# Chunk 2 of a delta-rule attention kernel: the products with the state issued ahead of the joins, and three smaller moves

## The chip, the cores and the metric

The kernel runs on one core of a Trainium2 chip. The metric is the device time of one execution in microseconds, here the median of ten runs. The engines work side by side, each in its own fixed order: TensorE (PE, with its weight loads shown as PEld), VectorE (DVE), ScalarE (ACT), GpSimd (POOL) and SyncE (SP), which issues most of the DMA transfers. ScalarE issues the transfers of the output. An engine goes on to its next instruction only when the one before it could start, so an instruction that waits holds back all that stand behind it.

## The reference

A delta-rule linear attention over 4 batches, 8 heads, 768 steps and a head size of 48, and behind it a two-layer feed-forward network on the 3072 rows of 8 x 48 = 384 values, with an inner size of 2048 and exact GELU:

```python
k_n = k / (np.linalg.norm(k, axis=-1, keepdims=True) + 1e-06)
state = np.zeros((B, H, D, D), dtype=np.float32)
for t in range(S):
    kt, vt, bt = (k_n[:, :, t], v[:, :, t], beta[:, :, t, None])
    y[:, :, t] = np.einsum('bhd,bhde->bhe', q[:, :, t], state)
    v_old = np.einsum('bhde,bhd->bhe', state, kt)
    state = state + bt[:, :, :, None] * np.einsum('bhd,bhe->bhde', kt, vt - v_old)
...
h = x @ w_in
g = 0.5 * h * (1.0 + erf(h * inv_sqrt2))
return (g @ w_out).astype(np.float32)
```

## The kernel before

The 768 steps are cut into 12 chunks of 64. Inside a chunk the recurrence is solved at once: with the Gram matrix of the chunk's keys, a triangular matrix of 64 x 64 per head is inverted, and the inverse Z is applied to what is left of the values once the state has been subtracted. Chunks go in pairs, called groups; group 1 is chunks 2 and 3. The 32 heads of a chunk lie in two units of 128 partitions (two batches each, `p`), 8 heads in the free direction.

**Inverse of a group.** `eliminate_steps` works on VectorE alone. The two 32 x 32 diagonal blocks of each triangle are eliminated in 30 steps of two instructions (L443, L445), in `Nu`. Three transpositions then lead back to the layout of the matmuls: the first (L454) into `XM`, the second and the third (both L458) into the columns 32 to 63 and 0 to 31 of `Zf`. The third is followed by four clearings on POOL (L470).

**Joins.** The off-diagonal block of each inverse is made by two small matmuls per head. `join_run` does a level 0 (off-diagonal Gram `G` times `XM`; VectorE scales the product by the step sizes `gm` and puts it back into `XM`, four instructions of L541) and a level 1 (`XM` times `Zf`; ScalarE copies it into `Zf`, four instructions of L512). `join_steps` makes three runs: the first joins are level 0 for the group's first chunk; the second are level 1 of the first chunk, in turn with level 0 of the second; the third are level 1 of the second.

**A chunk with the state.** `against_state` multiplies keys and queries of the chunk with the state (`psK`, L603; "K S" for the keys' part), copies the queries' part to `y` on ScalarE (L610) and forms `W` on VectorE: the keys' part less `V` (L611), times `gm` (L612). `solve` multiplies by Z (`psU`, L628) and ScalarE copies the result in eight pieces (L634). `use` makes the outputs and the change of the state (`psY`, L646 and L655), VectorE adds the change (L660) and forms `x` (L669), `turn` transposes `x` (`psX`, L690) for the network. `queries` is the product of queries and keys, masked by L403. `grams` makes the Gram matrix of a chunk (`psG`, L367) and has it copied into `G` and `diag`; for chunks above 3 these copies are put into a list by `put_off`, and `copy_out` issues them at a time of their own and holds them in the order of the program.

**The network** follows one chunk behind: `fc1` (`psH`, L713, with GELU on ScalarE, L715) and, for chunks 0 and 1, `fc2` (`psO`, L726); from chunk 2 on a second layer with seven products in place of eight (L751). It fills TensorE between the small matmuls of the next chunk. While chunk 2 of the attention is worked on, the network is at chunk 1.

**PSUM.** There are eight banks. `dn` is a buffer of two banks, there twice, for `psK`, `psU`, `psY`, `psG` and `psJ` of level 0. `mlp` is one bank, twice, for the network. From the end of chunk 1 on (`late`) there is one bank `sq`, for transposed blocks and `psJ` of level 1, and one bank `z`, used by one of the seven products (`psZ2`, L773). A new tile in a buffer waits until the last reader of the tile before it is done.

**Order.** A list `plan` gives each step a time on a scale in units of chunks; `at` spreads a list of steps over an interval, and `emit` issues all steps by time. VectorE keeps exactly this order (`manual_schedule`). A scheduler reorders the other engines by its own estimates, but for what `together` binds: it makes the matmuls of its steps follow each other without a break. For chunk 2, the plan has the elimination of group 1 with its three transpositions at 1.75 to 2.45, the three runs of joins at 2.64 to 2.77, the query products at 2.725, and the steps with the state at 2.76 to 2.985.

**Loads.** The keys of a chunk are loaded once whole as `Kn` (for the sum of squares, `ksq` on ScalarE, L278, and its reduction on VectorE, L281), once as blocks `Kb` (transposed on VectorE into `Kt`, L352), and once as `Kp`. Each load waits until the buffer's last reader is done, and the loads of SyncE go out one behind the other.

Of the kernel before, what the change touches and what calls it, by code (L numbers as in the profile page):

```python
# [8 lines left out]
F32 = mybir.dt.float32  # L9
# [7 lines left out]
def kernel(  # L17
# [28 lines left out]
    nc = tc.nc  # L46
# [6 lines left out]
    NA = B // 2  # L53
# [15 lines left out]
    def dn(name):  # L69
        return ps.tile([128, 2, 512], F32, tag="dn", name=name)  # L70

    def sq(name, *shape):
        return small[0].tile([128, *shape], F32, tag="sq", name=name)
# [17 lines left out]
    tiles = {}  # L91
# [149 lines left out]
    def decode_steps(first, last):  # L241
        def start_(n):
            begin(n)
            exponents(n)

        steps = [(0.6, start_, first), (1.5, mantissas, first)]
        for n in range(first, last):
            if n + 1 < last:
                steps += [(0.6, start_, n + 1), (1.9, signed, n), (1.5, mantissas, n + 1)]
        return steps + [(1.9, signed, last - 1)]  # L250
# [121 lines left out]
    def grams(us):  # L372
        g = us[0].c // 2
        psG = products(us, 0)
        if us[0].t == 0:
            Gs[g] = (wk if g else su).tile([128, NU, HB], F32, tag="G", name="G", bufs=1)
        span = slice(us[0].t * H, (us[-1].t + 1) * H)
        put = put_off if us[0].c > 3 else lambda name, dst, src: nc.scalar.copy(dst, src)
        put("gram", heads(Gs[g][:, span]), psG[:, :, :, HB:C])
        if g > 0:  # L380
            if us[0].t == 0:
                Ds[g] = wk.tile([128, NU, HB], F32, tag="diag", name="diag", bufs=1)
            put("gram", heads(Ds[g][:, span]), psG[:, :, :, 0:HB])
            for p in range(2):
                lower = slice(p * C + HB, (p + 1) * C)
                put("gram", Ds[g][lower, span], Gs[g][lower, span])
# [128 lines left out]
    def join_run(g, ts0, ts1):  # L515

        xm, zf, off = XMs[g], Zf[g % 2], Gs[g]
        gm = gms[g].rearrange("q t h -> q (t h)")
        sets = []
        for level, ts in enumerate((ts0, ts1)):  # L520
            if ts:
                psJ = sq("psJ", 512) if level else dn("psJ")[:, 0]
                sets.append((level, ts[0] * H, psJ.rearrange("q (k n) -> q k n", n=2 * HB)))
        for k in range(H):
            for p in range(2):
                for level, u0, psJ in reversed(sets):
                    us = slice(u0 + 2 * k, u0 + 2 * k + 2)
                    rows = slice(p * C + level * HB, p * C + (level + 1) * HB)
                    nc.tensor.matmul(psJ[HALF[p], k, :],  # L529
                                     lhsT=(xm if level else off)[rows, us, :],  # L530
                                     rhs=zf[rows, us, HB:C] if level else xm[rows, us, :],
                                     start=True, stop=True)
        for level, u0, psJ in sets:
            for p in range(2):
                for e in range(2):
                    us = slice(u0 + e, u0 + 2 * H, 2)
                    at_ = p * C + e * HB
                    src = psJ[at_:at_ + HB, :, e * HB:(e + 1) * HB]
                    if level == 0:
                        low_ = slice(p * C + HB, (p + 1) * C)  # L540
                        nc.vector.tensor_tensor(  # L541
                            xm[low_, us, :], src,
                            gm[low_, us].unsqueeze(2).to_broadcast([HB, H, HB]), op=ALU.mult)
                    else:
                        put_off("join", zf[p * C:p * C + HB, us, HB:C], src)
# [41 lines left out]
    def against_state(us):  # L587

        for u in us:
            u.W = wk.tile([128, H, D], F32, tag="W", name="W")  # L590
            u.y = None
            if u.c == 0:
                nc.gpsimd.tensor_tensor(u.W, u.V,
                                        ng[:, u.a].unsqueeze(2).to_broadcast([128, H, D]),
                                        op=ALU.mult)
                continue
            u.psK = dn("psK")[:, :, 0:2 * NP * D].rearrange("q r (x j d) -> q x r j d", x=2, d=D)
            for x in range(2):
                for j in range(NP):
                    for r, p in QUADS:  # L600
                        rows = slice(r * C, r * C + D)
                        to = HALF[p ^ (j % 2)] if x and u.c > 1 else HALF[p]
                        nc.tensor.matmul(u.psK[to, x, r, j, :], lhsT=(u.Qt if x else u.Kt)[rows, p, j, :],  # L603
                                         rhs=St[rows, u.a, p, j, :], start=True, stop=True)
        for u in us:
            if u.c == 0:
                continue
            gm = gms[u.c // 2][:, u.t]
            u.y = wk.tile([128, H, D], F32, tag="y", name="y")
            nc.scalar.copy(heads(u.y), u.psK[:, 1])  # L610
            nc.vector.tensor_tensor(heads(u.W), u.psK[:, 0], heads(u.V), op=ALU.subtract)  # L611
            nc.vector.tensor_tensor(u.W, u.W, gm.unsqueeze(2).to_broadcast([128, H, D]),  # L612
                                    op=ALU.mult)
# [226 lines left out]
    def at(first, last, steps):  # L840

        total, done, timed = sum(s[0] for s in steps), 0.0, []
        for w, *step in steps:
            timed.append((first + (last - first) * (done + 0.5 * w) / total, step))
            done += w
        return timed
# [109 lines left out]
    def late():  # L956
# [3 lines left out]
        for a in range(NA):  # L960
# [3 lines left out]
            for c in range(5, NC, 2):  # L964
                tiles[c, a].Kb = Kb

    plan = [at(c + 1 + 0.25 * (c == 1), c + 2 + 0.25 * (c == 0), ffn_steps(c)) for c in range(NC)]
    plan += [at(0.985, 1.26, decode_steps(3, n_in)), at(1.26, 1.65, decode_steps(n_in, NW)), at(1.66, 1.67, [(1.0, late)])]
    plan += [at(0.98, 0.985, [(1.0, load, 3)]),
             at(1.02, 1.1, [(1.0, join, 0, range(NA, 2 * NA), level) for level in range(2)]),  # L970
]
    sums = [(1.0, sum_of_squares, tiles[c, a], h) for c in (2, 3) for a in range(NA) for h in range(H)]
    plan += [at(1.08, 1.5, sums), at(1.51, 1.511, [(1.0, prep, c) for c in (2, 3)]), at(1.65, 1.655, [(1.0, finish_both)]), at(2.97, 2.971, [(1.0, finish, 4)]), at(2.725, 2.726, [(1.0, queries, third)]),
             at(1.12, 1.6, state_steps(1)),
             at(1.75, 2.45, eliminate_steps(1)),
             at(2.64, 2.77, [s for j in join_steps(1) for s in ((1.0, together, j), (0.0, copy_out, "join", 4))]), at(2.76, 2.985, state_steps(2)),
             at(2.72, 2.721, [(1.0, prep, 4)]), at(2.8, 2.9, [(1.0, grams, [tiles[4, a] for a in range(NA)]), (0.0, copy_out, "gram", 4)])]
    plan += [at(0.995, 1.0, [(1.0, load_v, 2)]), at(2.98, 2.981, [(1.0, sums_of_w)]), at(3.1, 3.11, [(1.0, last_sum_of_w)])]
    plan += [at(c - 0.4, c - 0.3, v_steps(c)) for c in range(4, NC)]
    plan += [at(2.08, 2.44, [(1.0, scale_head, tiles[c, a], h)  # L980
# [24 lines left out]
    for w in range(3, NC):  # L1005
        two_ahead = w + 2 < NC
        if w % 2:
            if w == 3:
                plan += [at(w + 0.09, w + 0.092, [(1.0, transposed, u, (1,)) for u in fourth]
                            + [(1.0, together, *gram(5))])]  # L1010
                plan += spread("gram", 4, w + 0.093)
            plan += [at(w + 0.25, w + 0.95, state_steps(w, (), query(w)))]
            if two_ahead:
                rows = eliminate_steps(w // 2 + 1)
                plan += [at(w - 0.16, w - 0.15, [(1.0, prep, w + 2)]),
                         at(w, w + 0.01, [(1.0, finish, w + 2)]),
                         at(w + 0.13, w + 0.18, rows[:2]), at(w + 0.18, w + 0.36, rows[2:14]),
                         at(w + 0.4, w + 1.06, rows[14:-3]), at(w + 1.07, w + 1.2, rows[-3:])]
        else:
            j0, j1, j2 = join_steps(w // 2)  # L1020
            plan += [at(w + 0.23, w + 0.232, [(1.0, together, j0, *query(w))]),
                     at(w + 0.3, w + 0.301, [(1.0, together, j1, *gram(w + 2))]),
                     at(w + 0.35, w + 0.97, state_steps(w, (j2,), gram(w + 3)))]
            plan += spread("join", 2, w + 0.32, w + 0.355)
            plan += spread("join", 4, w + 0.455)
            if two_ahead:
                plan += spread("gram", 1, w + 0.385, w + 0.42, w + 0.54, w + 0.58)
                plan += spread("gram", 1, w + 0.66, w + 0.661, w + 0.7, w + 0.701)
                plan += [at(w + 0.59, w + 0.591, [(1.0, prep, w + 2)]),
                         at(w + 0.9, w + 0.91, [(1.0, finish, w + 2)])]  # L1030
# [32 lines left out]
```

## Time and profile before

| | us |
|---|---|
| median of 10 runs | 661.91 |
| lowest and highest | 660.45, 663.54 |
| the profiled execution | 662.46 |
| its span in the profile | 660.7 |
| TensorE busy in the span | 634.9 |
| VectorE busy in the span | 457.3 |

The span goes from the first to the last instruction of the program; 1.8 us of the profiled execution lie around it. All times in the text below that are points on a line, such as "at 150.13", are microseconds from the start of the span. In the views an entry such as `128x256 f32 x24` counts instructions as the profiler sees them: an fp32 matmul of the program is two. An idle time in brackets at the end of a timeline's row is that before its first instruction, with the engine and line that ended it; `issue` means that the profile shows nothing that was waited for.

### The profile page before, as it was taken

The numbers are of one execution on the slowest core, as the hardware profiler recorded it, in microseconds if no ns is written. First come the engines' busy times: TensorE is split into PE (matmuls) and PEld (weight loads), VectorE is DVE, ScalarE is ACT, GpSimd is POOL, SyncE is SP. The second block draws the span as 40 slices with busy tenths as digits, with TensorE's granted clock in tenths as the row PEclk, the third lists the DMA queues.
The fourth block names the chain that finished last, engine by engine and source line by source line (L and its number), as shares of the span: only waits on it lengthen the run. The fifth ranks groups of instructions, "written<-read, shape, count | busy, mean of one in ns | idle before, by whom it ended". The sixth has DMA issues, their size and how long they took to land.

```text
span 660.7 us, 20457 instructions
## 1 busy us (share of the span) xinstructions
PE 634.9 (96%) x8902; PEld 558.1 (84%) x8902; DVE 457.3 (69%) x941; ACT 230.2 (35%) x625; POOL 80.2 (12%) x82
## 2 busy tenths in 40 slices
PE   6778999999999999999999999999999999999997
PEld 5666777766689989889989989989989989989997
DVE  6999999996789855778855778855778844325022
ACT  3367745613542136132136132136132133131220
POOL 4041300104111011301011301011301010000000
PEclk9965999999999999999999999999999999999999
DMA  9795655303523223521233510212300210100101
GB/s 138 161 267 162 128 151 162 49 0 53 86 37 60 52 37 53 94 39 20 55 39 52 98 36 20 50 20 41 60 17 18 52 16 3 25 2 2 24 1 25
DMA packets 158426, 39.68 MB, mean 60 GB/s; under 512 B 150016, under 2 KB 153216, under 8 KB 158336
## 3 DMA queue, kind: packets, MB, share of 16 engines
q1 hardware_dynamic: 152464, 33.40, 26.5%
q10 hardware_dynamic: 5872, 4.97, 3.3%
q8 instruction: 70, 1.15, 0.7%
q14 instruction: 20, 0.16, 0.1%
HBM read 33.62 MB, written 4.72 MB: 58 GB/s over the span
## 4 chain that ended last, share of the span: by engine, by line
PE 85%; DVE 9%; ACT 3%; issue 2%; DMA 1%; SPq 0%; ACTq 0%; DVEq 0%
PE psH L713 36%; PE psX L751 12%; PE psY L751 12%; PE psO L726 5%; PE psZ L751 4%; PE psK L603 3%; PE psG L367 3%; PE psJ L529 3%; PE psU L628 2%; PE psY L646 2%; DVE tmp L443 2%; DVE Nu L445 2%; PE psY L655 1%; DVE w_e L235 1%; ACT U L634 1%
## 5 line engine op out<-in xcount | busy, mean ns | idle before, releaser
L713 PE MATMUL psH<-xT,w_in_sb 128*128 128x256 f32 x1152 | 260.1, 384 | 2.7 <-ACT G L715 1.6
L713 PEld LDWEIGHTS psH<-xT,w_in_sb 128*128 128x128 f32 x1152 | 217.3, 191 | 34.7 <-ACT G L715 3.4
L715 ACT ACTIVATE G<-psH 128x256 f32<-128x256 f32 x192 | 73.2, 382 | 179.0 <-PE psH L713 161.8
L445 DVE TENSOR_TENSOR Nu<-Nu,tmp 128x30 f32<-128x30 f32 (+9 forms) x180 | 61.5, 341 | 6.2
L443 DVE TENSOR_TENSOR tmp<-Nu 128x30 f32<-128x30 f32 (+9 forms) x180 | 62.1, 345 | 5.0
L751 PE MATMUL psX<-w_out_sb,G 128*128 128x192 f32 x320 | 55.8, 328 | 0.0
L751 PE MATMUL psY<-w_out_sb,G 128*128 128x192 f32 x304 | 54.1, 330 | 1.1
L691 ACT COPY xT<-psX 128x384 f32<-128x384 f32 x24 | 11.4, 478 | 124.3 <-PE psX L690 123.6
L751 PEld LDWEIGHTS psX<-w_out_sb,G 128*128 128x128 f32 x320 | 52.4, 190 | 0.6
L751 PEld LDWEIGHTS psY<-w_out_sb,G 128*128 128x128 f32 x304 | 49.1, 190 | 3.2 <-DVE u L797 3.2
L760 DVE TENSOR_TENSOR S<-G 128x512 f32<-128x512 f32 x20 | 13.8, 691 | 45.9 <-ACT G L715 45.5
L306 POOL TENSOR_TENSOR n<-n,half 128x16 f32<-128x16 f32 x10 | 29.4, 2937 | 128.2 <-DVE n L281 107.9
L726 PE MATMUL psO<-w_out_sb,G 128*128 128x384 f32 x128 | 44.5, 493 | 0.0
L611 DVE TENSOR_TENSOR W<-psK,V 128x384 f32<-128x384 f32 x22 | 12.2, 554 | 36.7 <-ACT y L610 36.7
L726 PEld LDWEIGHTS psO<-w_out_sb,G 128*128 128x128 f32 x128 | 23.5, 190 | 14.1 <-DVE w_out_sb L236 0.5
L634 ACT COPY U<-psU 64x192 f32<-64x192 f32 x96 | 30.0, 312 | 9.4 <-PE psU L628 8.3
L470 POOL MEMSET Zf<- 32x512 f32 x23 | 12.4, 540 | 160.4 <-DVE Zf L458 159.4
L765 DVE TENSOR_TENSOR G<-G 128x512 f32<-128x512 f32 x20 | 13.8, 692 | 25.7 <-PE psX L751 25.7
L669 DVE TENSOR_TENSOR x<-psY,y 64x192 f32<-64x192 f32 x80 | 28.2, 353 | 0.9
L751 PE MATMUL psY<-T,G 128*128 128x192 f32 x160 | 28.2, 330 | 0.0
L751 PE MATMUL psZ<-T,S 128*128 128x192 f32 x160 | 28.1, 329 | 0.0
L751 PE MATMUL psX<-T,G 128*128 128x192 f32 x160 | 28.1, 329 | 0.0
(141 smaller groups left out, 860.0 us busy)
## 6 DMA issues: line engine op xcount, KB each, us to landing
Kp<-in_k_dram SPq DMA_DIRECT2D x76, 96.0 KB, 3.2
w_out_sb<-in_moe_w_in_dram SPq DMA_DIRECT2D x24, 256.0 KB, 4.0
V<-in_v_dram SPq DMA_DIRECT2D x48, 96.0 KB, 3.1
out_dram<-o_sb ACTq DMA_DIRECT2D x46, 96.0 KB, 2.2
w_raw<-in_moe_w_out_dram SPq DMA_DIRECT2D x10, 384.0 KB, 4.9
Zf<-in_moe_w_out_dram SPq DMA_DIRECT2D x6, 384.0 KB, 3.8
Qp<-in_q_dram SPq DMA_DIRECT2D x64, 32.0 KB, 2.1
Qp<-in_q_dram SPq DMA_DIRECT2D x16, 96.0 KB, 4.3
```

The costliest lines, as they stand in the source:

```text
L306: nc.gpsimd.tensor_tensor(flat, flat, half, op=ALU.pow)
L367: nc.tensor.matmul(psG[HALF[p], r, i * NP + j, :], lhsT=u.Kt[rows, p, j, :], rhs=(u.Qt if x else u.Kt)[rows, p, j, :], start=True, stop=True)
L443: nc.vector.tensor_tensor(tmp, nu[:, j + 1:, j:j + 1].to_broadcast([128, n, j]), nu[:, j:j + 1, 0:j].to_broadcast([128, n, j]), op=ALU.mult)
L445: nc.vector.tensor_tensor(nu[:, j + 1:, 0:j], nu[:, j + 1:, 0:j], tmp, op=ALU.add)
L529: nc.tensor.matmul(psJ[HALF[p], k, :], lhsT=(xm if level else off)[rows, us, :], rhs=zf[rows, us, HB:C] if level else xm[rows, us, :], sta ...
L603: nc.tensor.matmul(u.psK[to, x, r, j, :], lhsT=(u.Qt if x else u.Kt)[rows, p, j, :], rhs=St[rows, u.a, p, j, :], start=True, stop=True)
L634: copy(pairs(u.U[HALF[p]], s), u.psU[HALF[p ^ s], p])
L669: nc.vector.tensor_tensor(dst, src, pairs(u.y[HALF[p ^ s]], s), op=ALU.add)
L713: nc.tensor.matmul(psH, lhsT=w_in_sb[:, f // 2, m, f % 2 * 128:(f % 2 + 1) * 128], rhs=xTs[c][:, m, :], start=(m == 0), stop=(m == NM - 1))
L715: nc.scalar.activation(G[:, f, :], psH, ACT.Gelu)
L726: nc.tensor.matmul(u.psO, lhsT=G[:, f, u.a * 128:(u.a + 1) * 128], rhs=w_out_sb[:, f, :], start=(f == 0), stop=(f == NF - 1))
L751: nc.tensor.matmul(ps_, lhsT=lhs[:, f, :], rhs=rhs[:, f, :], start=first and f == 0, stop=f == FH - 1, skip_group_check=not first)
```

## The change

Five things change, all but the second in chunk 2's part of the plan or next to it.

1. `against_state` is cut in two. For chunk 2 it only issues its matmuls, at 2.6 of the plan's scale, ahead of the first joins; the copies to `y` and the forming of `W` become a function `subtract`, called at 2.711.
2. `psJ` of level 0 is put into the bank `z` in place of a `dn` buffer, in all groups that use `join_run`.
3. The third back transposition of group 1 (the second L458, with the clearing on POOL) is issued behind the first joins with their L541 (2.661), at 2.662.
4. The second and third joins are at 2.7 and 2.75, and the sums of squares of chunk 4 at 2.73; the rest of the steps with the state follow from 2.8.
5. The copies of the Gram matrices of chunks 4 and 5 are no longer put off: they are issued where the Gram matrix is made, and the scheduler places them.

```diff
-        put = put_off if us[0].c > 3 else lambda name, dst, src: nc.scalar.copy(dst, src)
+        put = put_off if us[0].c > 5 else lambda name, dst, src: nc.scalar.copy(dst, src)
...
-                psJ = sq("psJ", 512) if level else dn("psJ")[:, 0]
+                psJ = small[0].tile([128, 512], F32, tag="sq" if level else "z", name="psJ")
...
                         nc.tensor.matmul(u.psK[to, x, r, j, :], lhsT=(u.Qt if x else u.Kt)[rows, p, j, :],
                                          rhs=St[rows, u.a, p, j, :], start=True, stop=True)
+        if us[0].c != 2:
+            subtract(us)
+
+    def subtract(us):
+
         for u in us:
             if u.c == 0:
                 continue
...
+    rows1, join1 = eliminate_steps(1), join_steps(1)
...
-             at(1.75, 2.45, eliminate_steps(1)),
-             at(2.64, 2.77, [s for j in join_steps(1) for s in ((1.0, together, j), (0.0, copy_out, "join", 4))]), at(2.76, 2.985, state_steps(2)),
-             at(2.72, 2.721, [(1.0, prep, 4)]), at(2.8, 2.9, [(1.0, grams, [tiles[4, a] for a in range(NA)]), (0.0, copy_out, "gram", 4)])]
+             at(1.75, 2.43, rows1[:-1]),
+             at(2.66, 2.661, [(1.0, together, join1[0])]),
+             at(2.662, 2.663, rows1[-1:]),
+             at(2.6, 2.601, [(1.0, together, (against_state, third))]),
+             at(2.71, 2.711, [(1.0, subtract, third)]),
+             at(2.7, 2.701, [(1.0, together, join1[1]), (0.0, copy_out, "join", 4)]),
+             at(2.75, 2.751, [(1.0, together, join1[2]), (0.0, copy_out, "join", 4)]),
+             at(2.8, 2.985, state_steps(2)[1:]),
+             at(2.73, 2.731, [(1.0, prep, 4)]), at(2.8, 2.9, [(1.0, grams, [tiles[4, a] for a in range(NA)])])]
...
-                plan += spread("gram", 4, w + 0.093)
```

## The prediction

> **What bounds the kernel now.** I read the page first (which engine fills the span), then the busy times in short stretches around chunk 2, the only place where the built order of TensorE differs, then the timelines of TensorE and VectorE there, and last the waits. The page:
>
> ```profile
> PE 634.9 (96%) x8902; PEld 558.1 (84%) x8902; DVE 457.3 (69%) x941; ACT 230.2 (35%) x625; POOL 80.2 (12%) x82
> ...
> PE 85%; DVE 9%; ACT 3%; issue 2%; DMA 1%; SPq 0%; ACTq 0%; DVEq 0%
> ```
>
> TensorE is the bound: 96% busy, 85% of the chain that ended last. No matmul is added or taken away, so only idle TensorE time can be won. By stretches (us, then PE, PEld, DVE, ACT, POOL, granted clock, DMA share, GB/s):
>
> ```profile
> 140.00:145.00 5.00, 5.00 (x17) 3.01 (x16) 4.59 (x14) 0.00 (x0) 0.00 (x0) 1.00 0.00 0
> 145.00:150.00 5.00, 3.50 (x39) 1.88 (x37) 4.96 (x5) 0.00 (x0) 0.68 (x2) 1.00 0.00 0
> 150.00:155.00 5.00, 4.71 (x150) 3.39 (x152) 3.34 (x9) 1.93 (x5) 1.39 (x3) 1.00 0.01 3
> 155.00:160.00 5.00, 5.00 (x144) 3.59 (x142) 2.68 (x4) 2.84 (x7) 2.90 (x1) 1.00 0.49 95
> ...
> 175.00:180.00 5.00, 4.58 (x24) 3.83 (x23) 4.90 (x5) 1.69 (x5) 1.13 (x2) 1.00 0.70 132
> ```
>
> Between 145 and 150 us TensorE loses 1.5 us while VectorE is full. The timelines of TensorE and then VectorE show why (a matmul of the program counts as two here):
>
> ```profile
> 138.03 7.90 PE L726 MATMUL psO<-w_out_sb,G 128*128 128x384 f32 x24
> 145.86 1.15 PE L529 MATMUL psJ<-XM,G 32*64 32x64 f32 x32
> 146.94 1.56 PE L726 MATMUL psO<-w_out_sb,G 128*128 128x384 f32 x4
> 150.13 0.23 PE L529 MATMUL psJ<-Zf,XM 32*64 32x64 f32 x1 [1.64 <-issue]
> ```
>
> ```profile
> 143.53 2.08 DVE L454 STREAM_TRANSPOSE XM<-Nu 128x1024 f32<-128x1024 f32 x1
> 145.51 3.65 DVE L458 STREAM_TRANSPOSE Zf<-Nu 128x1024 f32<-128x1024 f32 x2
> 149.19 1.74 DVE L541 TENSOR_TENSOR XM<-psJ,gm 32x256 f32<-32x256 f32 x4
> 152.46 1.74 DVE L541 TENSOR_TENSOR XM<-psJ,gm 32x256 f32<-32x256 f32 x4 [1.52 <-PE psJ L529]
> 160.06 0.56 DVE L611 TENSOR_TENSOR W<-psK,V 128x384 f32<-128x384 f32 x1 [2.35 <-ACT y L610]
> ```
>
> The first joins end at 147.0, but VectorE reads them (L541) only behind both Zf transpositions (3.65 us). The second joins need half of that reading, so TensorE, out of queued work at 148.5, stands until 150.13: 1.64 us. It does K S only at 158.32. That is the idle time at stake.
>
> **TensorE, step by step.** From the start of the psO run at 138.03 to the first psY at 167.90 takes 29.87 us. Costs, start to start: 16 psO at full flow 5.16 (112.17 to 117.33), so 0.32 each; 8 psO between small matmuls 2.78 (155.54 to 158.32), 2 of them 0.85 (151.24 less 150.39), so a run between islands of small matmuls costs 0.2 more than its flow; 4 then 1.49. First joins 1.08, second 0.26 and 1.07, query products with third joins 1.31+1.07 (0.2 of it waiting), K S 2.01, Gram with U 2.01. Lines are named as in the kernel before. Built with the change, TensorE runs: 16 psO (5.20), K S (2.01), 8 psO (2.78), first joins (1.08), 4 psO (1.49), one second join (0.2), 2 psO (0.85), the other second joins (1.07), 8 psO (2.78), query products (1.10), third joins (1.07), 2 psO (0.85), U (1.0), 8 psO (2.78), Gram (1.1), 8 psO (2.78). Sum 28.1, so psY at 166.2: 1.7 us earlier, if nothing on the way waits.
>
> **Does anything wait?** First joins come 2.2 us later than now, at 148.0, for K S is ahead; XM is ready at 145.6. VectorE has one Zf transposition done at 147.4 and idles until 149.2, so its first L541 starts just where it starts today; moving the transposition alone hastens nothing. What changes is that K S fills TensorE meanwhile. L541 ends its upper half at 150.1 (TensorE arrives at 150.6) and all at 150.9 (TensorE at 151.6). Then the third transposition (1.89) runs 150.9 to 152.8, beside the second joins, which end at 152.8: today's 1.52 us of VectorE waiting takes it. Second L541 152.8 to 154.6, L611 and L612 to 156.8 (0.59+0.48+0.58+0.48, spacing today). Queued behind them: the query products need a psK bank pair, now free when the first L611 ends, at 155.2; TensorE arrives at 155.5. This is the new wait, with 0.3 us to spare. U needs the last L612 (156.8) and POOL's clearing of Zf, 2.23 us behind the transposition (155.1); TensorE arrives at 158.5. The Gram of chunk 4 needs mask (1.22), two n reductions and both Kt transpositions behind W: 160.2; it comes at 162.3. ScalarE: y copies at once, third-join copies 157.7 to 159.2, two ksq to 160.2, eight U copies (2.58) to 162.8, Gram copies to 164.6; psY asks for U at 166.2, the second psY for the Gram's bank at 167.3. POOL: its clearing starts 3.6 us later, with the two powers of n (2.9 each) queued behind it, ended by 164.8; L265 wants the first at about 172, behind chunk 5's Kt. All covered. Were VectorE 0.5 us later than worked out, 0.2 us would show.
>
> Weighed against a rule: each run between islands costs 0.2 us above flow, and splitting Gram from U makes one island more; that 0.2 is in the sum. [...]
>
> **SyncE and ScalarE behind.** The moves shift DMAs too. At 178.5 TensorE waits 0.42 for G, because ScalarE's queue stood on a DMA:
>
> ```profile
> 178.69 0.52 ACT L278 ACTIVATE ksq<-Kp 128x384 f32<-128x384 f32 x1 [2.18 <-DMA Kb<-in_k_dram]
> 179.12 0.64 ACT L715 ACTIVATE G<-psH 128x256 f32<-128x256 f32 x2
> ```
>
> and the 44 psH from 182.12 take 9.91 against 9.50 at flow (24 in 5.18), 0.4 more. In the change the V loads (waiting for L611) come first on SyncE, 155.2 to 157.8; one Kp half waits for its ksq to 159.7; the 16 block loads into Qp wait for Kt at 159.6 and follow at 0.5 each, with one or two 1.1 us hiccups as in 164.57 to 170.37: over at 169.3 to 170.4. Four Kp loads (0.65 each), then the other half of the first ksq's Kp, issued 171.9 to 174.1 and landing 3.1 to 3.8 us on: 175.0 to 177.9. The last Kp of the second ksq lands 1.3 later. ScalarE now has the first ksq behind two G, the second behind a Qt copy. TensorE starts psH of chunk 2 at 172.8 and wants that Qt copy at 178.3. It is there at landing plus 1.6: 176.6 to 179.5, so a wait of 0 to 1.2 replaces today's 0.42; I take 0.2 (landing near 176.9), for the loads start from an event known to 0.5 us. The 0.4 after it, from Gram and diag copies ahead of G, stays: the untied Gram copies are as many and as long (0.59 and 0.62 each), and the built ScalarE order has chunk 5's where they were. Bounds of this part: +0.4 to -0.8.
>
> **Costed at nothing.** First joins in Z's bank for chunks 4 to 10: TensorE's later order is the same, the second joins still need L541, and at 233.46 the first joins start with no idle before them; Z's readers end with the chunk before. If that cover failed, four groups would each wait; bounds 0 to 0.3 each by the 0.35 us that psY now waits for L797 per chunk. Elimination of chunks 4 and 5 begins 1 to 2 us earlier, with diag; if diag came no earlier, VectorE's W still ends at 198.7 against U at 200.7, 2 us.
>
> **Sum.** 1.7 for the filled wait, 0.2 for the G wait: 1.9 us. The profiled execution is 662.46 (span 660.7 plus 1.8 around it), 0.55 above the median 661.91 of ten. Against the median: 660.0. A difference under 0.2% (1.3 us) this measurement can hardly tell from none.
>
> **Rivals.** (1) The loads eat it: for, ScalarE already waits 2.18 us for such a load and the chain passes SyncE at 173.9 to 175.7; against, their start lies at 159.6 by events that shift little. A landing at 178 to 179 makes waits of 1.3 to 2.3 in place of 0.4: gain 0 to 0.9, time 661.4. (2) It does not do what it says, and the stall only moves to the query products: the first L541 is no earlier than today and the transposition now lies inside VectorE's path to W. For: 0.3 us to spare there. Against: U has 1.7, and every step of that path is a measured row. Were W 1.5 us late, the wait would be 1.2 and the gain 0.7: 661.2. (3) Slower: the same ksq loads, landing after 180.3, hold ScalarE's queue with G and Qt behind it; 3.6 us of TensorE's wait, less 0.4, against 1.7 won, is 1.5 lost: 663.4. It decides from a landing at 178.8 on, 0.9 above my latest; a third hiccup would reach it, a fourth would make it measurable.
>
> **How the numbers follow.** Forecast 0.62 (659.3 to 660.7 by itself), loads eat it 0.18, stall moved 0.08, slower 0.12. Low end 659.1: 2.1 us from TensorE and G both, and 0.7 for the 0.4 after and small gaps at 154. High end 662.3 takes in both rivals near no gain and leaves out the slower one. The forecast and a sliver of it below 1.3 us: faster 0.59, same 0.29, slower 0.12.
>
> **What would show it.** Right: K S near 143.2, no idle over 0.5 us before the second joins, the second L541 behind one transposition at about 152.8, psY near 166.2, xT's psH near 172.8, and the later chunks shifted alike. Wrong: idle before the query products or U (VectorE late); ScalarE's ksq waiting on a load past 178 with psT or psH waiting for it; or psJ in chunks 4 to 10 waiting for Z.

## The result, and the profile after

The changed kernel takes 659.1 us (median of 12 runs, 658.84 to 659.55), the kernel before beside it 661.43 (41 runs, 660.19 to 663.54). The ratio is 0.9963, with a 95% interval of 0.9955 to 0.9972: 2.3 us, 0.4%, faster. The profiled execution took 658.93 us, with a span of 657.2.

From the page of the changed kernel, the busy times and the chain that ended last:

```profile
PE 632.9 (96%) x8902; PEld 556.2 (85%) x8902; DVE 457.1 (70%) x941; ACT 230.0 (35%) x625; POOL 80.6 (12%) x82
...
PE 86%; DVE 8%; ACT 2%; issue 1%; DMA 1%; SPq 0%; DVEq 0%
```

The work is the same, the bound too. The short stretches, in the columns of the prediction's table, have TensorE full throughout:

```profile
140.00:145.00 5.00, 5.00 (x139) 3.48 (x137) 4.66 (x13) 0.76 (x2) 0.00 (x0) 1.00 0.01 3
145.00:150.00 5.00, 5.00 (x45) 2.92 (x44) 3.13 (x5) 0.20 (x1) 0.00 (x0) 1.00 0.00 0
150.00:155.00 5.00, 5.00 (x82) 2.98 (x85) 4.83 (x8) 1.93 (x5) 2.07 (x4) 1.00 0.01 3
...
175.00:180.00 5.00, 5.00 (x86) 4.08 (x85) 4.83 (x8) 3.19 (x8) 0.00 (x0) 1.00 0.49 81
```

The timelines of TensorE and of VectorE in the changed kernel, where lines behind 603 are numbered 5 higher than before (psO is L731, W is L616):

```profile
137.31 5.32 PE L731 MATMUL psO<-w_out_sb,G 128*128 128x384 f32 x16
142.56 0.68 PE L603 MATMUL psK<-St,Kt 48*64 48x48 f32 x32
...
147.35 1.15 PE L529 MATMUL psJ<-XM,G 32*64 32x64 f32 x32
148.43 1.56 PE L731 MATMUL psO<-w_out_sb,G 128*128 128x384 f32 x4
149.91 0.32 PE L529 MATMUL psJ<-Zf,XM 32*64 32x64 f32 x2
...
152.09 2.85 PE L731 MATMUL psO<-w_out_sb,G 128*128 128x384 f32 x8
154.87 1.16 PE L367 MATMUL psG<-Qt,Kt 48*64 48x64 f32 x64
...
165.61 0.68 PE L651 MATMUL psY<-U,P 64*64 64x48 f32 x32
```

```profile
144.79 1.94 DVE L458 STREAM_TRANSPOSE Zf<-Nu 128x1024 f32<-128x1024 f32 x1
148.54 1.74 DVE L541 TENSOR_TENSOR XM<-psJ,gm 32x256 f32<-32x256 f32 x4 [1.81 <-PE psJ L529]
150.32 1.94 DVE L458 STREAM_TRANSPOSE Zf<-Nu 128x1024 f32<-128x1024 f32 x1
152.29 1.72 DVE L541 TENSOR_TENSOR XM<-psJ,gm 32x256 f32<-32x256 f32 x4
154.04 0.56 DVE L616 TENSOR_TENSOR W<-psK,V 128x384 f32<-128x384 f32 x1
```

K S stands where TensorE stood idle, the second joins follow without a gap, and VectorE now waits 1.81 us ahead of the first L541, off the path. From the long psO run (137.31) to the first psY (165.61) take 28.30 us in place of 29.87: 1.57 won.

But the span fell by 3.5. The first long psO run starts 0.72 earlier already, and up to 142 us every engine has the same instructions in the same order in both kernels; the 44 psH come 0.49 sooner after psY; and a further 0.74 falls out near 277 us. To see what of this is the change, I cut the twelve profiles of this study at landmarks of TensorE: (a) the start of the 16 psO of 112.17 in the kernel before; from there to (b) the first psY of chunk 2; to (c) the start of the 44 psH behind the Gram of chunk 5; to (d) K S of chunk 3; to (e) K S of chunk 4; to (f) K S of chunk 5. From there to the end all twelve take 368.93 to 368.97.

| kernel | a | b | c | d | e | f | median us |
|---|---|---|---|---|---|---|---|
| before | 112.17 | 55.73 | 14.23 | 9.90 | 55.24 | 44.54 | 661.43 |
| before, again | 112.34 | 55.74 | 13.85 | 9.90 | 55.25 | 43.80 | 661.83 |
| before, bank and Gram only | 111.93 | 55.78 | 14.07 | 9.90 | 55.24 | 43.80 | 661.44 |
| before, squares of a constant | 111.54 | 55.72 | 13.57 | 9.91 | 55.24 | 43.80 | 661.06 |
| after | 111.45 | 54.16 | 13.74 | 9.90 | 55.24 | 43.80 | 659.1 |
| after, again | 111.30 | 54.16 | 14.17 | 9.90 | 55.24 | 43.80 | 659.21 |
| after, Gram copies put off | 111.90 | 54.16 | 13.95 | 9.91 | 55.24 | 43.80 | 659.88 |
| after, no late transposition | 111.45 | 54.16 | 13.96 | 9.90 | 55.24 | 43.92 | 659.6 |
| after, K S not ahead | 111.74 | 54.27 | 14.20 | 9.90 | 55.30 | 44.09 | 660.12 |
| after, Gram copies spread | 112.09 | 54.16 | 13.90 | 9.69 | 56.50 | 43.80 | 660.87 |
| after, half transposition more | 112.15 | 55.04 | 14.07 | 9.90 | 55.24 | 43.80 | 660.25 |
| after, transposition twice | 112.35 | 57.46 | 13.57 | 9.90 | 55.24 | 43.80 | 661.9 |

b, d and e repeat to a few hundredths wherever the order of the instructions is the same, and of these only b differs between the two kernels. a and c differ by as much within either kernel as between the two, and f shows its 0.74 in one execution of the kernel before but not in the other.

### The profile page after: what moved, and what is told of

The parts are those of the page before. It is cut to its first block, busy times and chain, and to the rows that moved or that the text cites. A ratio compares the mean times of both kernels' runs of the same rounds, so it can differ in the third digit from the quotient of the medians.

```text
span 657.2 us, 20461 instructions
## 1 busy us (share of the span) xinstructions
PE 632.9 (96%) x8902; PEld 556.2 (85%) x8902; DVE 457.1 (70%) x941; ACT 230.0 (35%) x625; POOL 80.6 (12%) x82
## 4 chain that ended last, share of the span: by engine, by line
PE 86%; DVE 8%; ACT 2%; issue 1%; DMA 1%; SPq 0%; DVEq 0%
PE psH L718 37%; PE psX L756 12%; PE psY L756 12%; PE psO L731 5%; PE psZ L756 4%; PE psK L603 3%; PE psG L367 3%; PE psJ L529 3%; PE psU L633 2%; PE psY L651 2%; DVE Nu L445 2%; DVE tmp L443 2%; PE psY L660 1%; DVE w_e L235 1%; ACT U L639 1%
## 5 line engine op out<-in xcount | busy, mean ns | idle before, releaser
L731 PE MATMUL psO<-w_out_sb,G 128*128 128x384 f32 x128 | 44.8, 494 | 0.0
L616 DVE TENSOR_TENSOR W<-psK,V 128x384 f32<-128x384 f32 x22 | 12.2, 554 | 33.6 <-ACT y L615 33.6
L731 PEld LDWEIGHTS psO<-w_out_sb,G 128*128 128x128 f32 x128 | 23.4, 190 | 13.9 <-DVE w_out_sb L236 0.5
```

What stands on the lines that cost most here:

```text
L731: nc.tensor.matmul(u.psO, lhsT=G[:, f, u.a * 128:(u.a + 1) * 128], rhs=w_out_sb[:, f, :], start=(f == 0), stop=(f == NF - 1))
```

## The experiments

**The kernel before once more.** No edit; it tells what differs between two executions of the same program.

> The kernel before, unchanged, for a second profile of it. Theory (the part of the gain that the prediction lacked, 0.75 us near 277 us and 0.05 near 180, is a load landing late in front of a ksq on ScalarE, and how late differs from one execution to the next): the stretch from the first psO of the long run to the first psY is 29.9 us again within 0.1, the time from the start to that psO differs from 138.03 by up to 1 us, and the waits at 179.54 and 277.37 come out with other sizes, 0 to 1.5 us each. Rival (the waits are fixed by the order of the queues): both waits within 0.1 us of 0.42 and 0.47. Time 661.4, ratio 1.000.

Measured: 661.83 us, ratio 0.9997 [0.9986, 1.0008]. The stall of 1.64 us in chunk 2 is the same, b 55.74. The wait near 277 is gone. TensorE and ScalarE in the first profile of the kernel before:

```profile
277.37 14.51 PE L713 MATMUL psH<-xT,w_in_sb 128*128 128x256 f32 x66 [0.47 <-ACT xT L691]
...
275.49 0.53 ACT L278 ACTIVATE ksq<-Kp 128x384 f32<-128x384 f32 x1 [1.40 <-DMA Kp<-in_k_dram]
```

and in the second:

```profile
276.54 14.41 PE L713 MATMUL psH<-xT,w_in_sb 128*128 128x256 f32 x66
...
274.42 0.52 ACT L278 ACTIVATE ksq<-Kp 128x384 f32<-128x384 f32 x1 [0.51 <-DVE u L803]
```

The sum of squares stands in ScalarE's queue ahead of the copy into xT. Where it waits 1.40 us for its load, TensorE waits 0.47 for xT; where the load is there, it doesn't. So the 0.74 of stretch f belongs to an execution, not to a kernel.

**Without the late transposition.** Both Zf transpositions ahead of the first L541 again; K S stays ahead.

```diff
-             at(1.75, 2.43, rows1[:-1]),
+             at(1.75, 2.45, rows1),
...
-             at(2.662, 2.663, rows1[-1:]),
```

> The changed kernel with the third back transposition in its old place, right behind the second, so ahead of the first joins' reading; K S stays ahead of the joins. Theory (K S ahead fills TensorE, the moved transposition is worth nothing beside it, because the first joins end only when three transpositions are over): first L541 at 11.2 to 11.4 us after the first psO, as in the changed kernel (11.23), psY 28.2 to 28.4 after it (28.30), time within 0.3 us of the changed kernel, 659.1. Rival (the transposition's move is needed too): the second joins wait 1 to 1.9 us, psY 29.3 to 30.2 after the first psO, time 660.1 to 661.

Measured: 659.6 us (659.05 to 659.85), ratio 0.9959 [0.9944, 0.9974]; b is 54.16, that of the changed kernel. VectorE:

```profile
144.81 3.73 DVE L458 STREAM_TRANSPOSE Zf<-Nu 128x1024 f32<-128x1024 f32 x2
148.58 1.74 DVE L541 TENSOR_TENSOR XM<-psJ,gm 32x256 f32<-32x256 f32 x4
```

Both transpositions end as the first joins do, and the first L541 starts at 148.58 against 148.54. With K S ahead, the place of the third transposition is worth nothing.

**Without K S ahead.** The transposition stays late; K S and the forming of W go back behind the joins.

```diff
-        if us[0].c != 2:
-            subtract(us)
+        subtract(us)
...
-             at(2.6, 2.601, [(1.0, together, (against_state, third))]),
-             at(2.71, 2.711, [(1.0, subtract, third)]),
...
-             at(2.8, 2.985, state_steps(2)[1:]),
+             at(2.76, 2.985, state_steps(2)),
```

> The changed kernel with K S and the forming of W back behind the joins, the third back transposition still behind the first joins' reading, Z's bank and the untied Gram copies kept. Theory (either move by itself removes the wait of 1.64 us): first L541 starts right behind the second transposition, 1.8 us earlier than before (9.3 to 9.5 us after the first psO against 11.16), no idle over 0.4 us before the second joins, psY 28.1 to 28.5 after the first psO; time 659.4 to 660.2. Rival (K S ahead alone fills the wait): idle of 1.2 to 1.7 us ahead of the second joins stays or turns up at the third joins, psY 29.5 to 29.9 after the first psO, time 661.0 to 661.4.

Measured: 660.12 us (659.5 to 661.5), ratio 0.9972 [0.9957, 0.9988]. TensorE, then VectorE:

```profile
145.44 1.15 PE L529 MATMUL psJ<-XM,G 32*64 32x64 f32 x32
146.51 1.56 PE L730 MATMUL psO<-w_out_sb,G 128*128 128x384 f32 x4
148.00 0.32 PE L529 MATMUL psJ<-Zf,XM 32*64 32x64 f32 x2
```

```profile
145.10 1.90 DVE L458 STREAM_TRANSPOSE Zf<-Nu 128x1024 f32<-128x1024 f32 x1
147.03 1.74 DVE L541 TENSOR_TENSOR XM<-psJ,gm 32x256 f32<-32x256 f32 x4
```

The first L541 starts as the one transposition ends, 0.4 us behind the joins, and the second joins follow with no idle time: b is 54.27, 1.46 less than before. So the late transposition alone fills the gap almost as well as K S ahead does. The two parts are two ways to the same 1.5 us, and their gains don't add. Of the 0.5 between this median and the one above, its profile shows 0.11 in b, 0.24 in c, where TensorE waits 0.24 for G, and 0.17 in f; the ratios' intervals overlap, and c and f vary between executions.

**The bank and the Gram copies alone.** The kernel before with points 2 and 5 of the change:

```diff
-        put = put_off if us[0].c > 3 else lambda name, dst, src: nc.scalar.copy(dst, src)
+        put = put_off if us[0].c > 5 else lambda name, dst, src: nc.scalar.copy(dst, src)
...
-                psJ = sq("psJ", 512) if level else dn("psJ")[:, 0]
+                psJ = small[0].tile([128, 512], F32, tag="sq" if level else "z", name="psJ")
...
-                plan += spread("gram", 4, w + 0.093)
```

> The kernel before with only the first joins' bank changed to Z's and the Gram copies of chunks 4 and 5 untied. Theory (these two are worth nothing by themselves): psY 29.8 to 30.0 us after the first psO, time 661.4 within 0.4 us, ratio 0.9995 to 1.0005. Rival (freeing a dn pair or letting the copies go early carries a part of the 0.8 us behind psY): psY the same, but time 660.4 to 660.8.

Measured: 661.44 us, ratio 0.9991 [0.9977, 1.0005], b 55.78. The stall is where it was:

```profile
149.93 0.32 PE L529 MATMUL psJ<-Zf,XM 32*64 32x64 f32 x2 [1.67 <-DVE XM L541]
```

In chunk 2 these two points change nothing, and in the time nothing that is clear of the noise.

**The Gram copies put off again.** The changed kernel without point 5. Every engine then has the changed kernel's instructions in the same order, so this is also a second sample of it.

```diff
-        put = put_off if us[0].c > 5 else lambda name, dst, src: nc.scalar.copy(dst, src)
+        put = put_off if us[0].c > 3 else lambda name, dst, src: nc.scalar.copy(dst, src)
...
+                plan += spread("gram", 4, w + 0.093)
```

> The changed kernel with the Gram copies of chunks 4 and 5 put off again; the built order of instructions on every engine is that of the changed kernel. Theory (the edit on the Gram copies is worth nothing; what differs between executions ahead of 138 us is chance of the first loads): 659.1, between 658.8 and 659.6, first psO of the long run anywhere from 137.3 to 138.2 us, from there to the first psY 28.3. Rival (the untied copies hasten elimination): 659.5 to 660.0, with VectorE's flip of chunks 4 and 5 later against the Gram than in the changed kernel.

Measured: 659.88 us (658.89 to 660.54), ratio 0.997 [0.9958, 0.9982], b 54.16, a 111.90. The median is above the range that I gave and inside the rival's, but the rival's sign is missing: the transposition of diag (L435) starts 3.89 us behind its Gram's start, against 3.90 in the changed kernel. So 0.8 us between two kernels with the same order is the size of what a, c and f do.

**The squares of a constant.** The kernel before, its ksq of chunks 6 and 7 free of any load:

```diff
-        kd = u.Kn[:, :, 0:D]
+        kd = u.Kn[:, :, 0:D] if u.c not in (6, 7) else half[:, 0:1].unsqueeze(2).to_broadcast([128, H, D])
```

> The kernel before, but the sums of squares of chunks 6 and 7 read a resident constant (0.5) in place of K, so the step sizes and outputs of these chunks are not the reference's; ScalarE's two pairs of ksq then wait for no load. Theory (the waits of TensorE for G at 179.5, 0.42 us, and for xT at 277.4, 0.47 us with 0.3 more around it, are ScalarE's queue standing on the landing of K, which varies between executions; the kernel before pays 0 to 1.2 for it, some 0.4 in its median): 661.0 to 661.5, a gain of 0.3 to 0.8 on the kernel before of the same call, no wait of TensorE for G or xT near 179 and 277, and a smaller spread than its 3 us. Rival A (the waits come from the Gram and diag copies or the output DMAs in ScalarE's queue): same time and waits as before. Rival B (the spread lies in the first 50 us): no waits there, but the same median within 0.3 and the same spread.

Measured: 661.06 us (660.33 to 662.58) beside 662.16 for the kernel before, ratio 0.999 [0.998, 1.0001]. c falls to 13.57, and TensorE waits for neither G near 179 nor xT near 277. ScalarE takes both pairs in one go (`half` is the constant, `Kp` a load):

```profile
162.18 0.98 ACT L278 ACTIVATE ksq<-half 128x384 f32<-128x384 f32 x2 [1.86 <-DVE n L281]
...
270.19 0.98 ACT L278 ACTIVATE ksq<-Kp 128x384 f32<-128x384 f32 x2 [8.33 <-DVE n L281]
```

The edit reached the first pair as meant: it stood at 162.81 and 178.69, its second half waiting for a load. The pair near 277 it didn't reach. That one is chunk 8's and still reads its load, but comes some 5 us sooner, with no wait for a transfer: twelve Kp loads go out from 198.56 on, where the kernel before issues eight from 199.84 on. So the wait near 179 is gone without the load (in the run with the transposition twice, where the load landed in time, c is 13.57 as well), and near 277 an earlier load left none. What these waits cost in the median isn't settled (the interval reaches from 1.3 us to nothing), and with a spread of still 2.2 us they can't be its only cause.

**The Gram copies spread.** The changed kernel with the four copies of chunk 5 set between the GELUs:

```diff
-        put = put_off if us[0].c > 5 else lambda name, dst, src: nc.scalar.copy(dst, src)
+        put = put_off if us[0].c > 4 else lambda name, dst, src: nc.scalar.copy(dst, src)
...
+                plan += spread("gram", 1, w + 0.093, w + 0.12, w + 0.15, w + 0.151)
...
-                         at(w + 0.13, w + 0.18, rows[:2]), at(w + 0.18, w + 0.36, rows[2:14]),
+                         at(w + (0.152 if w == 3 else 0.13), w + 0.18, rows[:2]), at(w + 0.18, w + 0.36, rows[2:14]),
```

> The changed kernel with the four Gram and diag copies of chunk 5 spread between the GELUs of the 44 psH, one, one and two. Theory (the 44 psH take 9.90 us start to start where flow is 9.50, because two of these copies stand ahead of a GELU): 9.5 to 9.6, so 0.3 to 0.4 less, 658.7 (658.5 to 659.1); diag comes 0.5 to 1.0 us later, which VectorE's 2 us of slack ahead of U of chunk 3 takes. Rival A: the psH wait for something else there, 9.9 and 659.1. Rival B: elimination ends later and the joins of chunks 4 and 5 wait: 659.5 to 660.0.

Measured: 660.87 us (660.17 to 662.11), ratio 0.9982 [0.9971, 0.9992], above all that was expected and 1.0 above the run with the Gram copies put off, which has the changed kernel's order and was measured beside it. The 44 psH lose half of their 0.4 (d 9.69), but e grows by 1.26. VectorE, then TensorE:

```profile
183.86 1.98 DVE L435 STREAM_TRANSPOSE Nu<-diag 128x1024 f32<-128x1024 f32 x1 [1.50 <-ACT diag L512]
...
216.93 0.36 DVE L799 TENSOR_TENSOR u<-psY,p 128x192 f32<-128x192 f32 x1
```

```profile
217.35 2.87 PE L756 MATMUL psY<-w_out_sb,G 128*128 128x192 f32 x16 [1.00 <-DVE u L799]
```

Elimination starts 1.1 later against the first psO than in the changed kernel (where the same transposition waits 0.44 for diag), and VectorE's order is full from there to 217 us: TensorE waits for u. The joins of the rival weren't late; another wait came first.

**The late transposition twice.** 1.94 us more on VectorE between the two L541, in the changed kernel:

```diff
-                nc.vector.transpose(Zf[g % 2][:, :, cols].rearrange("q u i -> q i u"), nu)
+                for _ in range(2 if (x, g) == (2, 1) else 1):
+                    nc.vector.transpose(Zf[g % 2][:, :, cols].rearrange("q u i -> q i u"), nu)
```

> The changed kernel with the late back transposition done twice, 1.94 us more on VectorE between the two readings of joins. Theory (the prediction's: the query products follow the end of the first L616 with some 0.3 us to spare, measured 0.27): second L541 at 154.2, W at 156.0, query products 1.6 to 1.7 us later than in the changed kernel, with TensorE idle ahead of them, all later work shifted by as much: 660.7 to 660.9. Rival (more slack than worked out, for the query products need no psK bank that is still held, or a later wait takes the same time in any case): 659.1 to 659.9.

Measured: 661.9 us (661.2 to 663.96), ratio 1.0003 [0.999, 1.0015]. TensorE waits where the theory says, but b grows by 3.30, not by 1.7. TensorE, and then the short stretches of TensorE alone (length, busy time, granted clock, DMA share, GB/s):

```profile
157.55 1.16 PE L367 MATMUL psG<-Qt,Kt 48*64 48x64 f32 x64 [1.70 <-DVE W L617]
158.64 1.32 PE L530 MATMUL psJ<-Zf,XM 32*64 32x64 f32 x32
159.88 1.65 PE L732 MATMUL psO<-w_out_sb,G 128*128 128x384 f32 x2
161.46 1.77 PE L634 MATMUL psU<-W,Zf 64*64 64x48 f32 x64
163.16 2.85 PE L732 MATMUL psO<-w_out_sb,G 128*128 128x384 f32 x8
```

```profile
158.50:159.00 0.50, 0.50 (x28) 1.00 0.07 13
159.00:159.50 0.50, 0.50 (x24) 0.97 0.88 159
159.50:160.00 0.50, 0.50 (x11) 0.50 0.57 73
...
162.50:163.00 0.50, 0.50 (x32) 0.62 0.09 12
163.00:163.50 0.50, 0.50 (x17) 1.00 0.09 16
```

The granted clock is 0.5 from 159.47 to 162.88. In it the third joins take 1.24 start to start in place of 1.08, two psO 1.58 in place of 0.84, U 1.70 in place of 1.08: 1.52 us that no wait shows.

**Half a transposition more.** The same with half of it done again, to part the wait from the clock:

```diff
+                if (x, g) == (2, 1):
+                    nc.vector.transpose(Zf[g % 2][:, :, 0:HB // 2].rearrange("q u i -> q i u"), nu[:, 0:HB // 2])
```

> The changed kernel with half of the late back transposition done a second time, some 0.75 us more on VectorE between the two readings of joins. Theory (a wait of TensorE at the query products equal to the delay less the 0.27 to spare; the further 1.52 us that the doubled transposition cost came from the granted clock of 0.5 after the longer stand): wait of 0.45 to 0.55 there, granted clock 1.00 throughout 156 to 164 us, all later work 0.5 later, 0.4 to 0.6 above the changed kernel of the same call. Rival A (small products alone are enough for the low clock): clock 0.5 in a stretch of 3.4 us again and 1.5 to 2 us more. Rival B (the delay is met by other slack): no wait, the time of the changed kernel.

Measured: 660.25 us (659.63 to 660.86), ratio 0.9978 [0.9969, 0.9986], 1.04 above the changed kernel beside it. TensorE, the half on VectorE, and a stretch with all engines as in the prediction's table:

```profile
156.45 1.16 PE L367 MATMUL psG<-Qt,Kt 48*64 48x64 f32 x64 [0.80 <-DVE W L618]
...
152.99 1.06 DVE L460 STREAM_TRANSPOSE Zf<-Nu 128x512 f32<-128x512 f32 x1
```

```profile
156.00:160.00 4.00, 3.55 (x134) 2.87 (x138) 3.93 (x7) 1.23 (x4) 0.40 (x1) 1.00 0.63 127
```

The half took 1.06, not the 0.75 I had estimated. The wait is that less the 0.27 to spare, 0.80; the clock stays at 1.00, and b grows by 0.88. So a delay of VectorE beyond 0.27 goes straight into the time here; of the 3.30 that the doubled transposition added to b, 1.70 was the wait and 1.52 the longer times in the stretch at 0.5.

**The changed kernel again**, on another chip, without an edit.

> The changed kernel itself, on another chip. Theory (the change is worth 1.57 us in chunk 2 and some 0.2 in the stretch up to the 44 psH; the start of the first psO, 111.45 to 112.35 us, and the stretch before the psH of 277 us, 0 to 0.74 of wait, differ from execution to execution in both kernels): first psO to psY of chunk 2 again 54.16 against 55.73, median 659.1 to 659.9, ratio 0.996 to 0.998. Rival (the changed order also makes the start-up shorter): first psO again at 111.45 within 0.1 and 659.1 within 0.2.

Measured: 659.21 us (658.67 to 660.41), ratio 0.9964 [0.995, 0.9977]; b 54.16 once more, a 111.30, c 14.17. The median and the ratio are within 0.11 us and 0.0001 of the first ones, and a is the lowest of all twelve. The order can't have made it so: up to 142 us it is that of the kernel before.

No variant beat the changed kernel. The bank in `z` couldn't be left out of it to test K S ahead alone: psK would hold both `dn` buffers until the first W, which stands behind the L541 that reads psJ, and each would wait for the other. It was not tried.

## Where the prediction failed, and what of it held

The direction, the mechanism and the main term held; the forecast of 660.0 was 0.9 too high. The step that failed is the sum: it had two terms, chunk 2 and the G wait, and put all else at nothing (the start without a word, the rest by "the later chunks shifted alike"), on a base of ten runs. By the medians, 0.48 of the 0.9 is the base: 661.91 from ten runs, 661.43 from 41 (and 661.48 to 662.16 in the samples taken later). The other 0.43 is the gain, 2.33 in place of 1.9. The two terms together are worth 1.6 to 1.7 us in the profiles, so they were not put too low; 0.6 to 0.7 us of the gain lies outside them, where the sum had nothing. That the low end of the range, 659.1, meets the result is luck: it counted on winning the 0.4 of the 44 psH, and they stayed (d is 9.90 in both kernels).

The same by the two profiled executions: the forecast was 662.46 less 1.9, 660.56; it took 658.93. The difference of 1.63 is, by stretches:

- **The filled wait, 1.7 forecast, 1.57 measured.** K S at 142.56 (143.2 forecast, less the 0.72 of the earlier start), the second L541 at 152.29, the query products 0.27 behind the end of the first W (0.3 forecast). The parts of the sum that were short are 0.05 in the first psO, 0.06 in the first second joins, 0.08 in U and the rest rounding. 8 psO between islands took 2.78 again (152.09 to 154.87), so the 0.2 above flow stands.
- **"Moving the transposition alone hastens nothing"** was right only with K S ahead. Alone it hastens the first L541 by 1.7 us (147.03 less 137.60, against 149.19 less 138.03) and wins 1.46.
- **The G wait, 0.2 forecast, 0.49 measured in the two profiles.** The landing was at 176.3, inside the forecast's 175.0 to 177.9, and no wait was left. In two other executions of the same order, the changed kernel again and the Gram copies put off, TensorE does wait there, 0.41 and 0.19 for Qt, as the forecast's 0 to 1.2 allowed. c is 13.85 to 14.23 in three profiles of the old order and 13.74 to 14.17 in five of the new one that keep it (after, again, put off, spread, half more), means of 14.05 and 13.97: as a property of the change it is 0.1, less than its scatter.
- **Near 277, nothing forecast, 0.74 measured.** "The later chunks shifted alike" failed as a reading of two profiles. The kernel before had paid for a late ksq load there; I had seen that ScalarE's queue stood on such a load at 178.7 and didn't look for the next one.
- **The start, nothing forecast, 0.72 measured.** a is 111.54 to 112.34 in the four profiles of the old order, 111.30 to 112.35 in the eight of the new one.

0.13 less, and 0.29, 0.74 and 0.72 more, make the 1.63 (rounded). So the range, built from the terms of the change, left out how far one execution lies from another, nearly a microsecond at the start and up to 0.7 at a ksq load.

What stays open: b and c make 1.6 to 1.7 us, while three comparisons of the same order give ratios of 0.9963, 0.9964 and 0.997, 2.0 to 2.4 us. In the profiles the rest lies in a and f, which favour the changed kernel on the mean (in f, no wait in any profile with K S ahead but 0.12 in one); how often the kernel before pays there, one profile per run can't tell.

A rival is on record too, in the mean granted clock of each execution. The kernel before has 88 executions with it. The 40 at 0.983 and more have a median of 661.35 us, the 28 at 0.979 to 0.982 one of 662.25, the 20 below 662.21 (of the four samples that make them up, one, of 12, has no such step). In the two samples of the changed kernel the same three groups have 659.1, 659.09 and 659.12 us, from 8, 3 and 9 executions. That would fit a stand of 1.64 us that in some executions is followed by a stretch at a granted clock of 0.5, as in the run with the transposition twice; filling it would then win more than b shows, and narrow the spread. It is not shown: in all four profiles with the stand, the granted clock is 1.00 from 146 to 158 us.

Of the rivals of the prediction, loads eating the gain didn't happen: after psY no stretch grew. The stall moved to the query products only where VectorE was given more work, in the runs with half a transposition more and with it twice, past the 0.27 us found to spare. The cover that the forecast named for a late diag, 2 us ahead of U of chunk 3, isn't the one that counts: 1.1 us of delay already made TensorE wait 1.00 for u at 217 us.

## What to carry to other kernels

When two edits each remove the same wait, test each alone: here either is worth the whole 1.5 us. Before a gain of a few tenths of a per cent is put down to a change, cut several executions of both kernels at the same landmarks: here stretches that follow the order of the instructions repeated to a few hundredths of a microsecond (b is 55.72 to 55.78 in four profiles), and those with a wait for a load didn't (c is 13.57 to 14.23). The slack of an engine that is full for 33 us, as VectorE in the run with the Gram copies spread, is set by the tightest reader in all that time, not by the nearest one: 1.1 us of delay made TensorE wait 1.00 at 217 us.

## What was not expected of the hardware

In the profile with the transposition twice, the stand of 1.70 us was not all that was lost: the granted clock was 0.5 from 159.47 to 162.88, beginning 1.9 us after work had resumed, and the third joins, two psO and U took 1.52 us more than in the changed kernel. The stands of 1.62 to 1.67 us in the four profiles of the old order left the granted clock at 1.00 (146 to 158 us), as did the one of 0.80 with half a transposition more (150 to 164 us). What sets the one apart from the others is not shown. The executions with the doubled transposition fall into four of 662.53 to 663.96 and six of 661.2 to 661.96; only the profiled one, of 662.98, was seen, and what parts the two groups is not shown either.
